# Thirty-two output products of a windowed attention, issued at steps from a table instead of in clusters of four

## The chip, the cores and the metric

The kernel runs on one core of a Trainium2 chip. The metric is the device time of one execution in microseconds (us), the median of several runs. TensorE (PE in the profile; PEld are its weight loads) multiplies, VectorE (DVE), ScalarE (ACT) and GpSimd (POOL) compute elementwise, and SyncE (SP) issues nearly all DMAs. Each engine works through its own queue in the order in which the program gave it the instructions.

## The reference, cut to what matters

Two attentions over 2048 positions, 576 columns and 32 heads of 18, whose outputs stand side by side. A looks at eight positions, two apart; B looks at all. All tensors are float32.

```
def _A_ref(x, wqkv, wo):
    q, k, v = ...                       # x @ wqkv, 32 heads of 18
    idx = pos[:, None] - (arange(8) * 2)[None, :]
    logits = einsum("bhsd,bhswd->bhsw", q, k[idx]) * scale     # masked where idx < 0
    o = einsum("bhsw,bhswd->bhsd", softmax(logits), v[idx])
    return o.reshape(1, 2048, 576) @ wo
def _B_ref(x, wqkv, wo):
    p = softmax(einsum("bhqd,bhkd->bhqk", q, k) * scale)
    return einsum("bhqk,bhkd->bhqd", p, v).reshape(1, 2048, 576) @ wo
return concatenate([a, b], axis=-1)
```

## The kernel before, in words

**Two stages.** In the first, some 415 us, the projections x @ wqkv of both attentions are made. The second is a loop over 512 steps, which this text numbers 0 to 511 as the kernel does. It is B's attention: 8 groups of 4 heads, each with 4 blocks of 512 query positions, make 32 blocks, and a block has 16 steps, one for each tile of 128 keys. So step 16m is the first step of block m.

**One step on each engine.** `score` makes four score matmuls (L229), one for each head, into four PSUM banks that are used in turn (the ring "scores"), and ScalarE takes each through exp into SBUF (L235). Beside three of the four, on the other half of TensorE's rows, runs a matmul of a "maximum" piece (L159), for a later block, into one of three other banks (the ring "else"); VectorE reduces each to its maximum (L166). The order of the pieces alternates: in odd steps they stand beside heads 0, 1 and 2, in even ones beside 0, 1 and 3. When all pieces of a block are done, VectorE makes one more reduction (`least`, L173). Then `weigh` multiplies the exps of the step before with the values and adds them up in the PSUM tile `po` (L701), which holds the sums of a whole block: its first group starts the sum anew, its last one ends it.

**The end of a block.** The sums of the block that ends are complete in step 16m, as `weigh` is one step late. There `finish` has ScalarE copy `po` to SBUF (L710). That copy stands in ScalarE's queue behind the four exps of step 16m and ahead of those of step 16m+1, and the first `weigh` of the next block, in step 16m+1, waits for it. What follows is put on an agenda of later steps: the denominators go out by DMA in step 16m+1 (`den<-o`, L733), VectorE inverts them in step 16m+8 (L734), they go to DRAM (`drec<-den`, L735) and back spread over rows (`rec<-drec`, L736, step 16m+13), and GpSimd multiplies (L737, step 16m+18), rounds and subtracts (L738, L739).

**Attention A beside it.** A is worked through in eight parts of 256 positions (`local(j)`, j from 0 to 7), each of which starts 54 steps after the one before, at step 10 + 54j; times within a part are counted from that step. `arrange` (L822) rearranges q, k and v in DRAM by three large DMAs of many small rows, for j = 4 at the steps 206 to 208. `fetch` (L830) loads them. GpSimd makes the logits in nine turns of a multiplication and an addition (L841, L845) and one last addition (L848). VectorE takes the maximum over the window in three halvings (`am`, L859, due at 31, 32 and 33), GpSimd subtracts it (L865), ScalarE makes the exps (L868, due at 35), VectorE sums them in three halvings (`as`, also L859, due at 36, 37 and 38) and inverts the sums (L875), GpSimd multiplies (`share`, L878, due at 39) and then weighs the values in nine turns (L884 to L887). The result goes to DRAM (`put`) and comes back turned (`get`, L909 and L911, six DMAs into the tiles `at0`, `at1` and `ahl`, of each of which there is one).

**The output products.** For each part, `get(n)` loads one of two tiles of 128 positions, and for each there are two products with `wo`, of 288 columns each: 32 in all. `finished(h)`, when its agenda step p comes, puts the product on the list `inside`, and the scores loop takes it from there in step p + 1, ahead of head 2 or head 3. A product (`sums_of_a`, which calls `beside`) is 27 matmuls in pairs on the two halves of the rows (L1010) with two more maximum pieces in between; it takes one bank of each ring. Then ScalarE copies one of its two sums to the tile `y` (L927) and VectorE adds the other (L928). Six steps after its second product's agenda step, a tile is stored.

Of the kernel before, what the change touches and what calls it, by code (L numbers as in the profile page):

```python
# [43 lines left out]
GAP = 54  # L44

A_FROM = 10


def ap(t, *dims):
# [4 lines left out]
def rows(t, *dims):  # L54

    return bass.AP(tensor=t.tensor, offset=t.offset, ap=[list(d) for d in dims])
# [3 lines left out]
def two_attentions(ctx: ExitStack, tc, xa, wa, woa, xb, wb, wob, out):  # L60
# [53 lines left out]
    def plan(start, pieces):  # L114
        for n, f in pieces:
            agenda[start + n].append(f)
# [222 lines left out]
    with (tc.tile_pool(name="x", bufs=1, side="right") as xp,  # L339
# [104 lines left out]
        if True:  # L444
# [195 lines left out]
            for k in range(2, 14):  # L640
                n = 46 if k == 2 else 36 + 4 * k
# [7 lines left out]
            def leave_a(c, b, n, ps):  # L649
                o = xp.tile([128, 512], F32, name="ohi", bufs=4)  # L650
                nc.scalar.activation(o[:n], ps, AF.Copy)  # L651
                load(da[128 * c : 128 * c + n, HALO + 512 * b : HALO + 512 * b + 512], o[:n])
# [23 lines left out]
            for c, b in order:  # L676
                n = min(128, 3 * D - 128 * c)
                work_list.append(((b % 2, ws[c][0], xas[b][0], slice(0, n), every),
                                  lambda ps, n=n: ps[:n], lambda ps, c=c, b=b, n=n: leave_a(c, b, n, ps)))
# [135 lines left out]
    def local(j):  # L815
# [4 lines left out]
        def arrange(n):  # L820
            wide = (HALO if n else 0) + SUB
            load(rows(dparts[j][n][0, 0], (wide, D), (D * wide, 4), (1, wide)),  # L822
                 rows(da[D * n, HALO + p0 + SUB - wide :], (HALO + S, D), (SUB, 4), (1, wide)))


        def fetch(nm):
            halo = 0 if nm == "q" else HALO
            n = DH * (halo + SUB)
            t = st[nm] = work.tile([128, DH, halo + SUB], F32, name="akv" if halo else "aq", bufs=2 if halo else 1)
            load(ap(t, (1, n)), rows(dparts[j]["qkv".index(nm)][0, 0], (n, 128), (1, n)))  # L830
# [49 lines left out]
        def weighted(c):  # L880
            if c == 0:
                st["o"] = work.tile([128, DH, SUB], F32, name="ao", bufs=1)
            at = wide()
            nc.gpsimd.tensor_mul(at, ap(st["lg"], (0, 2), (SUB, W), (1, SUB)), window(st["v"], c))  # L884
            nc.gpsimd.tensor_add(at[:, :, :4], at[:, :, :4], at[:, :, 4:])  # L885
            nc.gpsimd.tensor_add(at[:, :, :2], at[:, :, :2], at[:, :, 2:4])
            nc.gpsimd.tensor_add(st["o"][:, 2 * c : 2 * c + 2], at[:, :, 0], at[:, :, 1])  # L887
# [10 lines left out]
        def put(i):  # L898
            load(rows(dao[j, i, 0, 0], (DH * SUB, 128), (1, DH * SUB)),
                 ap(st["parts"][i].bitcast(F32), (1, DH * SUB)))  # L900

        def get(n):
            st["x"] = []
            st["n"] = n
            last = work.tile([128, 128], F32R, name="ahl", bufs=1)
            for i in range(2):
                t = work.tile([128, 4, 128], F32R, name=f"at{i}", bufs=1)
                for s in range(2):
                    load(t.bitcast(F32)[:, :, SUB * s : SUB * s + SUB],  # L909
                         dao[j, i, 2 * n + s, :512].rearrange("(c p) n -> p c n", p=128))  # L910
                load(last.bitcast(F32)[64 * i : 64 * i + 64].rearrange("p (s n) -> p s n", s=2),  # L911
                     rows(dao[j, i, 2 * n, 512], (SUB, 64), (D * SUB, 2), (1, SUB)))
                st["x"].append([t[:, c] for c in range(4)])
            st["x"].append(last)

        def finished(h):
            inside.append(lambda: sums_of_a(h))

        def sums_of_a(h):
# [3 lines left out]
            if h == 0:  # L923
# [6 lines left out]
        pieces = [(0, lambda: fetch("q")), (1, lambda: fetch("k")), (28, lambda: fetch("v")), (33, lower),  # L930
                  (35, exponents), (39, share), (60, upper), (61, rest), (64, lambda: put(0)), (66, lambda: put(1))]
# [3 lines left out]
        for c in range(DH // 2):  # L935
            pieces.append((5 + 5 * c // 2, lambda c=c: match(c)))
            pieces.append((39 + 5 * c // 2, lambda c=c: weighted(c)))
        at = A_FROM + GAP * j - 24

        at = max(at, STEPS * (at // STEPS) + 14) - A_FROM - GAP * j  # L940
        for n in range(3):
            pieces.append((at + n if j else n - 7, lambda n=n: arrange(n)))
        for n, (at, ends) in enumerate(((70, (78, 80)), (81, (87, 89)))):
            pieces.append((at, lambda n=n: get(n)))
            for h in range(2):
                pieces.append((ends[h], lambda h=h: finished(h)))
                producing.add(A_FROM + GAP * j + ends[h] + 1)
            pieces.append((ends[1] + 6, lambda n=n: load(out[p0 + 128 * n : p0 + 128 * n + 128, :D], ys["a", j, n])))
# [141 lines left out]
    for j in range(NJ):  # L1090
        plan(A_FROM + GAP * j, local(j))
    for g in range(1, NG):
# [39 lines left out]
    while step < ALL:  # L1132
        n, kt = divmod(step, NT)
# [51 lines left out]
```

## Time and profile before

| what | value |
|---|---|
| time before, median of 3 runs | 1646.38 us (1645.86 to 1647.27) |
| time of the profiled execution | 1646.54 us |
| its span, first to last instruction | 1644.8 us |
| granted TensorE clock | 0.999 |
| busy: PE / DVE / ACT / POOL | 1633.1 / 1397.0 / 1221.9 / 959.2 us |

The time of the profiled execution is 1.74 us more than its span, and 0.16 us more than the median. The busy time of PE is modelled, so that a matmul that waits for a short while is not seen in it: how long a step takes is read better from the starts of successive L701 groups in the timeline, since each step has one. The timeline merges neighbouring instructions of one line; "x8" is one step's group, four matmuls that count twice each. In brackets behind a row stands how long the engine was idle before it, and what ended that.

### The profile page before, as it was taken

To read this page: it belongs to the slowest core of one execution; us is meant where nothing else is said; L and a number is where in the kernel's file an instruction comes from. 1 tells how busy PE (TensorE), PEld (TensorE's weight loads), DVE (VectorE), ACT (ScalarE), POOL (GpSimd) and SP (SyncE) were. 2 spreads that over 40 slices of the span, in tenths; PEclk is the share of its full clock that TensorE was granted. 3 is DMA by queue.
4 is the path that set the end of the run, shared out by engine and by line. 5 is a ranking of instruction groups with operands and counts; after the bars stand their busy time and mean duration, and the time that the engine had idled before them with its cause. 6 is when DMAs were issued, how large, how long until landed. Compare 5 with 4: busy or idle time off the path is not lost.

```text
span 1644.8 us, 33745 instructions
## 1 busy us (share of the span) xinstructions
PE 1633.1 (99%) x12906; PEld 935.0 (57%) x12906; DVE 1397.0 (85%) x2366; ACT 1221.9 (74%) x2419; POOL 959.2 (58%) x792
## 2 busy tenths in 40 slices
PE   9999999999999999999999999999999999999998
PEld 7999879998433444444344344344344344445676
DVE  5199989999899989889889899889899989888533
ACT  6314432111899998998998998998998998998554
POOL 2306642210195995994994994994995996940000
PEclk9999999999999999999999999999999999999999
DMA  8837955522515347157139325716526132033201
GB/s 252 238 113 204 257 165 140 134 87 90 95 48 100 98 120 135 54 139 143 53 93 161 82 77 130 147 65 122 134 79 117 65 107 78 21 114 123 101 37 59
DMA packets 188353, 188.22 MB, mean 114 GB/s; under 512 B 118384, under 2 KB 132208, under 8 KB 186464
## 3 DMA queue, kind: packets, MB, share of 16 engines
q1 hardware_dynamic: 183328, 174.53, 40.9%
q0 software_dynamic: 4032, 10.63, 3.0%
q8 instruction: 101, 1.65, 0.4%
q10 hardware_dynamic: 832, 0.92, 0.2%
q14 instruction: 60, 0.49, 0.1%
HBM read 113.16 MB, written 88.12 MB: 122 GB/s over the span
## 4 chain that ended last, share of the span: by engine, by line
PE 96%; DMA 2%; DVE 1%; ACT 0%; POOL 0%; issue 0%; SPq 0%; ACTq 0%; POOLq 0%; DVEq 0%
PE po L701 30%; PE bank L229 25%; PE bank L322 16%; PE bank L159 13%; PE bank L1010 7%; PE bank L259 5%; DMA den<-o 1%; DVE mx L166 1%; DMA dqk<-ohi 0%; POOL xlo L370 0%; DMA first<-xb 0%; DVE am L859 0%; SPq L363 0%; DMA out<-y 0%; PE bank L985 0%
## 5 line engine op out<-in xcount | busy, mean ns | idle before, releaser
L166 DVE TENSOR_REDUCE mx<-bank 128x1 f32<-128x512 f32 x2048 | 1288.1, 683 | 144.6 <-PE bank L159 115.8
L235 ACT ACTIVATE e<-bank 128x512 f32<-128x512 f32 x2048 | 1060.2, 613 | 94.3 <-PE bank L229 51.0
L159 PE MATMUL bank<-ks,qs 54*128 54x512 f32 x2048 | 752.7, 423 | 2.1 <-DVE mx L166 2.0
L229 PEld LDWEIGHTS bank<-qs,ks 56*128 56x128 f32 x2048 | 331.1, 186 | 454.1 <-ACT e L235 423.6
L229 PE MATMUL bank<-qs,ks 56*128 56x512 f32 x2048 | 582.0, 425 | 0.0
L701 PE MATMUL po<-e,v 128*19 128x512 f32 x4096 | 538.1, 599 | 0.0
L159 PEld LDWEIGHTS bank<-ks,qs 54*128 54x128 f32 x2048 | 340.8, 185 | 15.6 <-DVE mx L166 7.6
L841 POOL TENSOR_TENSOR pr<-aq,akv 128x1024 f32<-128x1024 f32 x72 | 158.4, 2201 | 28.1 <-DMA akv<-dpart 25.6
L701 PEld LDWEIGHTS po<-e,v 128*19 128x19 f32 x4096 | 70.6, 97 | 182.1 <-issue 171.4
L884 POOL TENSOR_TENSOR pr<-lg,akv 128x1024 f32<-128x1024 f32 x72 | 158.1, 2196 | 0.6
L845 POOL TENSOR_TENSOR pr<-pr 128x1024 f32<-128x1024 f32 x64 | 152.5, 2382 | 5.0
L651 ACT ACTIVATE ohi<-bank 128x512 f32<-128x512 f32 (+1 forms) x56 | 30.5, 595 | 148.3 <-issue 116.9
L322 PE MATMUL bank<-xlo,ahi 64*128 64x512 f32 (+1 forms) x448 | 117.9, 389 | 1.4 <-POOL xlo L370 1.4
L322 PE MATMUL bank<-xhi,alo 64*128 64x512 f32 (+1 forms) x448 | 116.1, 388 | 0.0
L322 PE MATMUL bank<-xhi,ahi 64*128 64x512 f32 (+1 forms) x448 | 113.7, 388 | 1.1 <-ACT ohi L651 1.1
L885 POOL TENSOR_TENSOR pr<-pr 128x512 f32<-128x512 f32 x72 | 92.3, 1282 | 5.6
L370 POOL TENSOR_TENSOR alo<-raw,ahi 128x512 fp32r<-128x512 f32 (+1 forms) x14 | 17.6, 1254 | 121.1 <-ACT ahi L369 86.7
L463 POOL TENSOR_TENSOR olo<-olo,ohi 128x512 fp32r<-128x512 f32 x36 | 46.1, 1294 | 63.8 <-ACT ohi L462 58.4
L737 POOL TENSOR_TENSOR o<-o,rec 128x512 f32<-128x512 f32 x29 | 37.2, 1284 | 64.3 <-DMA rec<-drec 35.4
L322 PEld LDWEIGHTS bank<-xlo,ahi 64*128 64x128 f32 (+1 forms) x448 | 67.2, 182 | 7.6 <-POOL xlo L370 2.5
L322 PEld LDWEIGHTS bank<-xhi,alo 64*128 64x128 f32 (+1 forms) x448 | 65.8, 182 | 5.3
L322 PEld LDWEIGHTS bank<-xhi,ahi 64*128 64x128 f32 (+1 forms) x448 | 63.8, 181 | 7.2 <-ACT ohi L651 1.5
(197 smaller groups left out, 1790.5 us busy)
## 6 DMA issues: line engine op xcount, KB each, us to landing
do<-n SPq DMA_DIRECT2D x28, 512.0 KB
da<-ohi SPq DMA_DIRECT2D x52, 256.0 KB
dpart<-da SPq DMA_DIRECT2D x16, 702.0 KB
akv<-dpart SPq DMA_DIRECT2D x16, 702.0 KB
out<-y SPq DMA_DIRECT2D x32, 288.0 KB
qs<-dqk SPq DMA_DIRECT2D x30, 288.0 KB
ks<-dqk SPq DMA_DIRECT2D x30, 288.0 KB
at<-dao SPq DMA_DIRECT2D x64, 128.0 KB
```

The costliest lines, as they stand in the source:

```text
L159: nc.tensor.matmul(ps, qs[at, b, p, 128 * t : 128 * t + 128], ks[at, p, 512 * k : 512 * k + 512], start=True, stop=True)
L166: nc.vector.tensor_reduce(mx[:, r, p, t, k : k + 1], ps, axis=AX.X, op=ALU.max)
L229: nc.tensor.matmul(ps, ks[at, p, 128 * kt : 128 * kt + 128], qs[at, b, p], start=True, stop=True)
L235: nc.scalar.activation(e, ps, AF.Exp, scale=SCALE)
L259: nc.tensor.matmul(ps, a, b, start=c == i == 0, stop=c == 4 and i == 1)
L322: nc.tensor.matmul(ps, a, b, start=start, stop=stop)
L701: nc.tensor.matmul(po[32 * i : 32 * i + 19], vs[g][:, kt, 19 * i : 19 * i + 19], es[i], start=kt == 0, stop=kt == NT - 1)
L841: nc.gpsimd.tensor_mul(pr, ap(st["q"][:, 2 * c], (SUB, 2), (0, W), (1, SUB)), window(st["k"], c))
L845: nc.gpsimd.tensor_add(st["pr"], st["pr"], pr)
L884: nc.gpsimd.tensor_mul(at, ap(st["lg"], (0, 2), (SUB, W), (1, SUB)), window(st["v"], c))
L885: nc.gpsimd.tensor_add(at[:, :, :4], at[:, :, :4], at[:, :, 4:])
L1010: nc.tensor.matmul(ps, a, b, start=start, stop=stop)
```

## The change

The four products of a part stood at fixed places, 78, 80, 87 and 89 steps after the part's start, with the loads at 70 and 81. Now their agenda steps are in a table, counted over the whole loop, one row for each part. Of its 32 entries 24 are a multiple of 16, so that these products run in step 16m+1: for m = 6 to 28 and m = 30. The load for a tile's products is due eight steps ahead of the first of them, or one step after the second product of the tile before, whichever is later. The steps that count as having two more maximum pieces (`producing`) and the store follow the table.

```
+MADE = ((88, 96, 112, 128), (144, 160, 176, 192), (201, 208, 224, 240), (250, 256, 272, 288),
+        (304, 320, 336, 352), (361, 368, 384, 400), (412, 416, 432, 448), (466, 468, 475, 480))
...
-        for n, (at, ends) in enumerate(((70, (78, 80)), (81, (87, 89)))):
-            pieces.append((at, lambda n=n: get(n)))
+        made = [p - A_FROM - GAP * j for p in MADE[j]]
+        for n, ends in enumerate((made[:2], made[2:])):
+            pieces.append((max(ends[0] - 8, made[1] + 1 if n else 0), lambda n=n: get(n)))
             for h in range(2):
                 pieces.append((ends[h], lambda h=h: finished(h)))
                 producing.add(A_FROM + GAP * j + ends[h] + 1)
```

Before, the products ran in the steps 89, 91, 98, 100 and then 54 steps later each time, up to 467, 469, 476 and 478. No instruction is added or removed: each engine's queue holds the same instructions in another order, and from step 489 on the order is as before.

## The prediction
> **What bounds the kernel now.** First the page: engines, and the chain of work that ended last.
>
> ```profile
> PE 1633.1 (99%) x12906; PEld 935.0 (57%) x12906; DVE 1397.0 (85%) x2366; ACT 1221.9 (74%) x2419; POOL 959.2 (58%) x792
> ...
> PE 96%; DMA 2%; DVE 1%; ACT 0%; POOL 0%; issue 0%; SPq 0%; ACTq 0%; POOLq 0%; DVEq 0%
> ```
>
> TensorE is the path almost throughout. As no matmul is added or removed, only time in which TensorE waits can come or go. Its busy time hides short waits, so I read the timeline of PE and took the distance between the starts of successive L701 groups as the length of a step. Around the end of block 7 (steps 112 to 114) it says:
>
> ```profile
> 667.39 1.05 PE L701 MATMUL po<-e,v 128*19 128x512 f32 x8
> 669.51 1.05 PE L701 MATMUL po<-e,v 128*19 128x512 f32 x8
> 671.81 1.05 PE L701 MATMUL po<-e,v 128*19 128x512 f32 x8
> ...
> 668.73 0.63 ACT L710 ACTIVATE o<-po 128x512 f32<-128x512 f32 x1
> 669.21 7.31 ACT L235 ACTIVATE e<-bank 128x512 f32<-128x512 f32 x14
> ```
>
> A plain step is 2.12 us; the one from 669.51 to 671.81, step 114 = 16·7 + 2, is 2.30. The second view, ScalarE over the same time, says why: the copy starts at 668.73 and the next exp at 669.21, so a queued activation takes 0.48 us of ScalarE. Four make 1.92, 0.2 less than a step. The copy puts ScalarE 0.48 late, one step gives back 0.2, and in the next TensorE waits for score banks. The first such step is 18 and the last 482:
>
> ```profile
> 456.42 1.05 PE L701 MATMUL po<-e,v 128*19 128x512 f32 x8
> 458.69 1.05 PE L701 MATMUL po<-e,v 128*19 128x512 f32 x8
> ...
> 1518.09 1.05 PE L701 MATMUL po<-e,v 128*19 128x512 f32 x8
> 1520.37 1.05 PE L701 MATMUL po<-e,v 128*19 128x512 f32 x8
> ```
>
> They are 2.27 and 2.28 long. Of the ends m = 1 to 30, 26 show it; 146, 210, 306 and 370 don't, as a product stood in step 16m or 16m + 1.
>
> **The copies.** Step 305 = 16·19 + 1 already has a product where the table puts 24:
>
> ```profile
> 1106.35 1.05 PE L701 MATMUL po<-e,v 128*19 128x512 f32 x8
> 1110.59 1.05 PE L701 MATMUL po<-e,v 128*19 128x512 f32 x8
> 1112.70 1.05 PE L701 MATMUL po<-e,v 128*19 128x512 f32 x8
> ...
> 1110.17 0.41 ACT L927 ACTIVATE y<-bank 128x288 f32<-128x288 f32 x1 [0.90 <-PE bank L1010]
> ```
>
> It takes 4.24 us and the step after it 2.11, a plain one. A product so adds 2.12 to its step, and ScalarE, with the copy behind it, still has 0.90 us idle ahead of the product's own copy. So there the copy of the sums is free. Six ends stay uncovered (m = 1 to 5 and 29): 20 stalls of 0.17 go, **−3.4 us**.
>
> On this size the Trainium skill speaks otherwise: its page "ScalarE: Activation LUTs" ("What ACT_TABLE_LOAD costs") gives an activation 186 ns and 0.833 ns an element, with 93 ns of overlap between neighbours, an estimate of 0.52 us for 512 elements. By that figure ScalarE would have 0.04 us to spare in a step, a copy would cost TensorE nearly all its time, and 20 would bring over 9 us, with a sum below of some −11 instead of −4.65; the spacing of 0.48 and the step of 2.30 decide against it.
>
> **GpSimd's lead.** Moving products changes how long other work has between two steps. For part 1, two products (steps 89, 91) stood between `share` of part 0 and `am` of part 1; now one.
>
> ```profile
> 625.97 1.28 POOL L848 TENSOR_TENSOR lg<-pr 128x512 f32<-128x512 f32 x1
> 632.72 1.29 POOL L865 TENSOR_TENSOR lg<-lg,am 128x512 f32<-128x512 f32 x1 [5.46 <-DVE am L859]
> ...
> 628.14 0.42 DVE L859 TENSOR_TENSOR am<-lg 128x256 f32<-128x256 f32 x1
> ...
> 526.80:627.20 100.40, 96.66 (x70) 1.00 0.39 101
> ```
>
> GpSimd works without a break from 526.8 to the end of the logits at 627.25 (in the last row, busy time by stretches: 96.66 of 100.4 with 70 instructions; the rest is small change between them), so that this end stays. VectorE reaches `am` at 628.14 now, and by one product's 2.12 earlier after: 626.02. It waits 1.2 us; behind `am` stand the reductions that free banks for the maximum pieces, so TensorE stops for most of it. I take **+1.15** (0.8 to 1.4). For the later parts three or four products lie in that stretch instead of two, so the lead grows.
>
> **The `as` step.** The first `as` halving comes in an odd step, where the third piece is early and VectorE has least to spare. Before, from part 1 on a product ran just ahead of it.
>
> ```profile
> 518.35 1.05 PE L701 MATMUL po<-e,v 128*19 128x512 f32 x8
> 520.63 1.05 PE L701 MATMUL po<-e,v 128*19 128x512 f32 x8
> ...
> 519.59 0.42 DVE L859 TENSOR_TENSOR as<-lg 128x256 f32<-128x256 f32 x1
> ...
> 641.82 1.05 PE L701 MATMUL po<-e,v 128*19 128x512 f32 x8
> 643.95 1.05 PE L701 MATMUL po<-e,v 128*19 128x512 f32 x8
> ```
>
> Part 0, without a product, pays 2.28 − 2.12 = 0.16; part 1, with it, nothing (2.13). After, all parts but 3 (product in 209) lose that cover: 6 × 0.16 = **+1.0** (0 to 1.0).
>
> **The long stall at step 218.** The largest wait of the loop is one DMA:
>
> ```profile
> 864.78 0.92 SPq L909 DMA_DIRECT2D at<-dao  x2
> ...
> 867.69 2.68 SPq L911 DMA_DIRECT2D ahl<-dao  x1
> ...
> 872.18 0.35 SPq L735 DMA_DIRECT2D drec<-den  x1
> ...
> 882.95 0.58 SPq L736 DMA_DIRECT2D rec<-drec  x1
> 883.59 12.82 SPq L822 DMA_DIRECT2D dpart<-da  x3
> 896.50 5.74 SPq L733 DMA_DIRECT2D den<-o  x1
> ...
> 909.99 0.25 DVE L734 RECIPROCAL den<-den 128x16 f32<-128x16 f32 x1 [2.44 <-DMA den<-o]
> ...
> 908.35 1.05 PE L701 MATMUL po<-e,v 128*19 128x512 f32 x8
> 912.46 1.30 PE L701 MATMUL po<-e,v 128*19 128x512 f32 x8
> 915.70 1.45 PE L701 MATMUL po<-e,v 128*19 128x512 f32 x8
> ```
>
> SP is blocked for 12.82 us by `arrange` of part 4, `den` of step 209 is issued behind it and lands at 909.99, VectorE stands, and TensorE loses 4.11 − 2.11 = 2.0 and 3.24 − 2.11 = 1.1, and 0.4 in the step after: 3.5. `arrange` itself waits for nothing that is computed; it starts late because `rec` stands ahead of it, which waits for `drec`, which SP reached only after the second load of part 2 (864.78 to 870.37). That load waited for the product in step 199. In the new table it is due at 216, after all this. SP then comes to `drec` when the inverse is made, some 3 us earlier against the steps, and its landing, with one load less ahead of it (128 × 576 values of 4 bytes, twice), comes earlier too. Against that, part 2's first load moves from 188 to 193, the very step of a product that it must wait for, and what SP has behind it is late. From both: the stall ends between nothing and its whole; I take **−2.2** (−3.5 to 0).
>
> **VectorE against GpSimd.** An `am` of 256 columns takes 0.42 (row at 628.14), but:
>
> ```profile
> 1002.30 1.37 DVE L859 TENSOR_TENSOR am<-lg 128x256 f32<-128x256 f32 x1
> ...
> 1002.11 1.28 POOL L737 TENSOR_TENSOR o<-o,rec 128x512 f32<-128x512 f32 x1 [5.35 <-DMA rec<-drec]
> ...
> 1003.34 1.05 PE L701 MATMUL po<-e,v 128*19 128x512 f32 x8
> 1006.19 1.05 PE L701 MATMUL po<-e,v 128*19 128x512 f32 x8
> ...
> 1376.77 1.06 PE L701 MATMUL po<-e,v 128*19 128x512 f32 x8
> 1382.04 1.05 PE L701 MATMUL po<-e,v 128*19 128x512 f32 x8
> ```
>
> It ends when GpSimd's multiplication does, and the step after it, 259 (1003.34 to 1006.19), is 2.85, 0.73 over. Step 422 (1376.77 to 1382.04), a product step with two late `am` halvings ahead of it, is 5.27 instead of 4.24: 1.03. In the first case the multiplication waited for `rec`, which SP issued behind a load whose product stood in step 253; that load is now due at 264, `rec` comes earlier, and the multiplication is over by then. In part 7 GpSimd is further ahead. I take two thirds of 1.76, **−1.2** (−1.8 to +1, as other meetings can form).
>
> **The sum.** −3.4 + 1.15 + 1.0 − 2.2 − 1.2 = −4.65. From the profiled 1646.54 that is 1641.9; this execution is 0.16 above the median, so I predict **1641.7**. The moved loads themselves I cost at nothing: seven of eight second loads are due eight steps (17 us) before their product, where 81 to 87 left six; if that cover were short, TensorE would wait for the landing.
>
> **Rivals.** A measurement of this kernel tells about 0.2% (3.3 us) from no change: below 1643.1 is faster, above 1649.7 slower.
>
> *The side effects eat it.* The copies go, but `den` stays as late and the meetings of VectorE and GpSimd only change place: −3.4 + 1.15 + 1.0 = −1.25, **1645.1**. For it: without the two uncertain gains the sum stays under the bound. Against it: the load that blocked SP is gone from that place. Chance 0.19.
>
> *The product doesn't cover the copy*, so the change doesn't do what it says: the product's own copy to `y` also runs on ScalarE in that step. Then the 3.4 stays: −4.65 + 3.4 = −1.25, **1645.1** too. Step 305 speaks against it. Chance 0.03.
>
> *SP late from step 193: slower.* The load due in 193 waits for that step's product, about 3 us, then issues for 5.6 (864.78 to 870.37), then come nine small DMAs at 0.35 or more (as `drec`), then `den` of block 12: some 12 us after the step's start. If the queue is then as full as at 896.50, where landing took 13.5 us from the issue, `den` lands at 25.5, and the inverse is wanted at 4.24 + 7 × 2.12 + 0.25 = 19.3. That is 6 us, and the stall at 218 stays: −1.25 + 6 = +4.75, **1651.1**. From 4.6 us late on it is past the bound. Against it: in the same queue, some steps later, such a load went out whole in 5.6 us and `drec` followed 1.8 us behind its end, so a queue as full as at 896.50 is not to be expected. Chance 0.10.
>
> **How the numbers follow.** My forecast has 0.68. The best of every term gives −3.4 + 0.8 + 0 − 3.5 − 1.8 = −7.9: low end 1638.5. The worst of the uncertain ones (1.4, 1.0, 0, +1) gives 0.0; the two rivals without change of sign lie at 1645.1, and 1646.0 takes them in and leaves out what is left of the upper side, with the third, some 0.15. Faster 0.68, within the bound 0.19 + 0.03 = 0.22, slower 0.10.
>
> **What would show it.** In the profile after: steps 16m + 2 for m = 6 to 28 and 30 at 2.11 and 16m + 1 at 4.23; a VectorE `am` of part 1 that starts where L848 ends, with some 1 us lost in steps 96 and 97; `den` of step 209 issued earlier against the steps; 0.16 at the first `as` of parts 1, 2, 4 to 7. Wrong would be: 2.28 still in those steps, or a long inverse (L734) wait anywhere, step 200 first.

## The result: 0.2% slower, and where it went

| kernel | time, median us | ratio to the kernel before, 95% interval |
|---|---|---|
| before | 1647.10 (14 runs) | |
| changed | 1651.01 (14 runs) | 1.0020 (1.0012 to 1.0029) |

The forecast was 1641.7, and 1638.5 to 1646.0: the change went the other way. The profiled execution of the changed kernel took 1651.53 us, its span is 1649.8 (1644.8 before).

I read its profile as the one before, by the starts of successive groups of the values' matmul (now L704; lines behind the table stand three or four further down). First the end of block 7, which the prediction showed with 2.30 us in step 114. The four rows are the steps 111 to 114, with a product in 113:

```profile
664.78 1.05 PE L704 MATMUL po<-e,v 128*19 128x512 f32 x8
666.89 1.05 PE L704 MATMUL po<-e,v 128*19 128x512 f32 x8
671.13 1.05 PE L704 MATMUL po<-e,v 128*19 128x512 f32 x8
673.23 1.05 PE L704 MATMUL po<-e,v 128*19 128x512 f32 x8
```

The product step takes 4.24 and the step after it 2.10: the copy costs nothing. So it is at all 24 ends that the table covers; the stall is left at 18, 34, 66, 82 and 466 (at 50 another wait took its place in step 49). The gain that the change was argued from is there in full.

Now the place of the longest stall, step 218, in the timeline of TensorE, then VectorE, then SP:

```profile
906.34 1.05 PE L704 MATMUL po<-e,v 128*19 128x512 f32 x8
916.25 1.91 PE L704 MATMUL po<-e,v 128*19 128x512 f32 x8
920.10 1.24 PE L704 MATMUL po<-e,v 128*19 128x512 f32 x8
922.39 1.05 PE L704 MATMUL po<-e,v 128*19 128x512 f32 x8
...
867.42 0.24 DVE L737 RECIPROCAL den<-den 128x16 f32<-128x16 f32 x1
...
913.23 0.25 DVE L737 RECIPROCAL den<-den 128x16 f32<-128x16 f32 x1 [7.66 <-DMA den<-o]
...
850.86 0.93 SPq L912 DMA_DIRECT2D at<-dao  x2
...
865.26 0.43 SPq L952 DMA_DIRECT2D out<-y  x1
...
872.62 0.35 SPq L738 DMA_DIRECT2D drec<-den  x1
...
887.79 0.57 SPq L739 DMA_DIRECT2D rec<-drec  x1
888.41 10.25 SPq L825 DMA_DIRECT2D dpart<-da  x3
898.76 7.56 SPq L736 DMA_DIRECT2D den<-o  x1
```

From 906.34 to 916.25 are 9.91 us, then 3.85 and 2.29: 9.7 us over three plain steps of 2.12, where the kernel before lost 3.5. VectorE waited 7.66 instead of 2.44 for `den` (the inverse at 867.42, of the block before, waited for nothing). TensorE lost more than VectorE waited, and the busy times by stretches say why; behind the length of the stretch the columns are PE, PEld, DVE, ACT and POOL, then TensorE's granted clock, the DMA engines' share and GB/s:

```profile
907.50:910.00 2.50, 0.32 (x1) 0.00 (x1) 0.00 (x0) 0.92 (x2) 2.34 (x3) 1.00 1.01 88
910.00:913.00 3.00, 0.00 (x0) 0.00 (x0) 0.00 (x0) 0.00 (x0) 2.84 (x4) 0.55 0.20 21
913.00:916.00 3.00, 1.92 (x6) 1.32 (x6) 2.77 (x6) 0.66 (x2) 2.84 (x4) 0.50 0.31 101
916.00:919.00 3.00, 3.00 (x13) 0.97 (x14) 1.09 (x3) 1.09 (x3) 2.92 (x2) 0.50 0.81 183
919.00:922.00 3.00, 3.00 (x19) 1.15 (x18) 2.00 (x4) 2.18 (x5) 2.84 (x4) 0.74 0.81 235
```

TensorE stood from about 908, its clock fell to half, and stayed there until about 920, six us after work came back. A group that takes 1.05 us elsewhere takes 1.91 at 916.25. The Trainium skill has this rule on its page "TensorE: Matmul & The Clock Gate" ("What's actually happening"): after an idle window of some 3.4 us the array gets half its clock, and only a busy window gives it back. The trace agrees on the half, 0.50, and on a return only after some six us of work. It doesn't show the idle window of 3.4 us: TensorE's last matmul ended at 907.82, and a mean of 0.55 over 910 to 913 puts the fall at some 910.3, 2.5 us later. The kernel before had the half clock too, shorter:

```profile
913.00:916.00 3.00, 3.00 (x19) 1.31 (x15) 2.21 (x5) 1.76 (x5) 2.84 (x4) 0.52 0.93 312
```

By steps 2 to 486 of the two profiled executions, over plain steps of 2.115 us and product steps of 4.23 and 4.21 (these are sums over the rows of L701 and L704):

| where | before | after | difference |
|---|---|---|---|
| ends of blocks that the table covers (20 stalls) | 3.4 | 0 | −3.4 |
| steps 212, 213, 259, 373, 422 | 3.0 | 0 | −3.0 |
| steps 218 to 220 | 3.5 | 9.7 | +6.2 |
| step 97 | 0 | 1.3 | +1.3 |
| steps 104 to 106 | 0.2 | 0.9 | +0.7 |
| first `as`, steps 101, 155, 263, 317, 425 | 0 | 0.9 | +0.9 |
| all others | 3.3 | 3.8 | +0.5 |
| sum | 13.4 | 16.6 | +3.2 |

The spans differ by 5.0. Some 1.6 of that came before the loop's second step, where the two kernels have the same instructions in the same order. Over the ten profiles of this study, all with that same first stage, step 2 begins between 422.7 and 426.7: that part is scatter of the single execution, and it isn't the change. The last 0.2 are the product steps themselves: before, about half of the 32 took 4.21 instead of 4.23, after it three.

Two more rows of the forecast's list. Part 1's `am` waits for the logits, 1.36 us, and the product step 97 (628.49 to 634.06) is 5.57 long:

```profile
628.49 1.05 PE L704 MATMUL po<-e,v 128*19 128x512 f32 x8
634.06 1.05 PE L704 MATMUL po<-e,v 128*19 128x512 f32 x8
...
629.05 0.43 DVE L862 TENSOR_TENSOR am<-lg 128x256 f32<-128x256 f32 x1 [1.36 <-POOL lg L851]
```

And a second `den`, of block 6, is late where the forecast named none; it was issued behind part 2's `arrange`:

```profile
651.17 1.05 PE L704 MATMUL po<-e,v 128*19 128x512 f32 x8
654.20 1.05 PE L704 MATMUL po<-e,v 128*19 128x512 f32 x8
...
651.73 0.25 DVE L737 RECIPROCAL den<-den 128x16 f32<-128x16 f32 x1 [1.08 <-DMA den<-o]
```

### The profile page after: what moved, and what is told of

It reads as the page before. It is cut to its first block, busy times and chain, and to the rows that moved or that the text cites. A ratio compares the mean times of both kernels' runs of the same rounds, so it can differ in the third digit from the quotient of the medians.

```text
span 1649.8 us, 33746 instructions
## 1 busy us (share of the span) xinstructions
PE 1632.9 (99%) x12906; PEld 951.6 (58%) x12906; DVE 1392.9 (84%) x2366; ACT 1224.0 (74%) x2419; POOL 960.1 (58%) x792
## 4 chain that ended last, share of the span: by engine, by line
PE 90%; POOL 6%; DMA 1%; DVE 1%; issue 1%; ACT 0%; SPq 0%; POOLq 0%; ACTq 0%; DVEq 0%
PE po L704 27%; PE bank L232 22%; PE bank L325 16%; PE bank L162 13%; PE bank L1014 7%; PE bank L262 5%; POOL pr L844 1%; POOL pr L887 1%; POOL pr L848 1%; DMA den<-o 1%; DVE mx L169 1%; POOL pr L888 1%; POOL pr L889 0%; DMA dqk<-ohi 0%; PE bank L478 0%
## 5 line engine op out<-in xcount | busy, mean ns | idle before, releaser
L232 PE MATMUL bank<-qs,ks 56*128 56x512 f32 x2048 | 573.0, 426 | 0.0
L704 PE MATMUL po<-e,v 128*19 128x512 f32 x4096 | 538.4, 600 | 0.0
L162 PEld LDWEIGHTS bank<-ks,qs 54*128 54x128 f32 x2048 | 341.3, 185 | 18.0 <-DVE mx L169 11.4
L704 PEld LDWEIGHTS po<-e,v 128*19 128x19 f32 x4096 | 70.6, 97 | 185.7 <-issue 182.9
L325 PE MATMUL bank<-xlo,ahi 64*128 64x512 f32 (+1 forms) x448 | 111.2, 390 | 0.2 <-POOL xlo L373 0.2
L325 PEld LDWEIGHTS bank<-xlo,ahi 64*128 64x128 f32 (+1 forms) x448 | 62.5, 183 | 3.2 <-POOL xlo L373 1.0
```

The source lines that it names most:

```text
L162: nc.tensor.matmul(ps, qs[at, b, p, 128 * t : 128 * t + 128], ks[at, p, 512 * k : 512 * k + 512], start=True, stop=True)
L232: nc.tensor.matmul(ps, ks[at, p, 128 * kt : 128 * kt + 128], qs[at, b, p], start=True, stop=True)
L325: nc.tensor.matmul(ps, a, b, start=start, stop=stop)
L704: nc.tensor.matmul(po[32 * i : 32 * i + 19], vs[g][:, kt, 19 * i : 19 * i + 19], es[i], start=kt == 0, stop=kt == NT - 1)
```

## The experiments

Two theories stood against each other. **Queue**: the change gains by the products' places and loses it all, and more, at `den` of step 209, which SP issues late because part 2's first load now waits in its queue for a product of its own step. **Spread**: products that stand alone cost more than products in clusters, and the stall at 218 is one of the forms this takes.

The ratios below are to runs of the kernel before that were made beside each run: their median is 1648.64 us (20 runs) for the first four kernels, which ran on one chip, and 1647.47 (23 runs) for the other four, on another.

**Part 4's `arrange` moved away from `den`, in both kernels.** In each, one line:

```
-        at = max(at, STEPS * (at // STEPS) + 14) - A_FROM - GAP * j
+        at = (180 if j == 4 else max(at, STEPS * (at // STEPS) + 14)) - A_FROM - GAP * j
```

In the changed kernel:

> The changed kernel with one more edit: the three DMAs of arrange for part 4 are due at steps 180 to 182 instead of 206 to 208, so that the denominators of step 209 are not issued behind them. Theory (queue): the whole loss of the change is the wait of VectorE for these denominators in step 218, 9.7 us of TensorE in the changed kernel (8.65 and 1.06 over a plain step) against 3.5 before. Then steps 218 and 219 are plain, TensorE's clock stays at 1.0 around them, and the time is 1651.0 - 9.7 = 1641.3 (1640 to 1643), 0.35% under the kernel before. Rival (moved, not removed): the DMA work is the same and another den, rec or load is late instead; the time stays at 1647 to 1651. Rival (spread): the products cost more where they stand now than in clusters, beside the stall; then 1644 or more.

Measured: 1640.54 us, 0.9956 of the kernel before (0.9941 to 0.9971). The steps 218 and 219 in its timeline are plain, and the clock is whole:

```profile
904.62 1.05 PE L704 MATMUL po<-e,v 128*19 128x512 f32 x8
906.73 1.05 PE L704 MATMUL po<-e,v 128*19 128x512 f32 x8
908.85 1.05 PE L704 MATMUL po<-e,v 128*19 128x512 f32 x8
...
910.00:915.00 5.00, 5.00 (x37) 2.25 (x37) 4.31 (x8) 4.85 (x10) 4.76 (x5) 1.00 0.03 12
```

In the kernel before:

> The kernel before with the same edit alone: arrange of part 4 at 180 to 182. Theory (queue): steps 218 and 219 lose their 3.5 us, 1647.1 - 3.5 = 1643.6 (1642.5 to 1645). The difference to the changed kernel with this edit is then what the change does beside that one stall: by the steps of its trace -3.4 (copies), +1.3 (step 97), +0.7 (step 106 against 104 and 105), +0.9 (as), -2.8 (steps 212, 259, 373, 422), about -3. Rival (moved): no change of time.

Measured: 1643.92 us, 0.9969 (0.9959 to 0.9980). With that one stall out of both, the changed kernel is 3.4 us below the kernel before, on the same chip and about as its steps add up (8.1 over plain, against 11.9). The intervals of the two ratios overlap, so the size of this gain rests on the steps as well as on the medians. With that, the change's other effects are a gain, and the stall at 218 turns it. The rival "moved, not removed" falls for the changed kernel, in whose trace no other step took the stall over. In the kernel before the time falls too, but its trace has a wait that wasn't there: VectorE waits 1.61 us for a later `den`, and step 282 loses 1.2. As the profiled execution was the slowest of the nine (1646.78), it stays open whether this wait belongs to the edit.

**The product ahead of part 2's first load.** One entry of the table:

```
-        (144, 160, 176, 192)
+        (144, 160, 176, 184)
```

> The changed kernel with one table entry changed, 192 to 184: the first load of part 2 stays due at 193, but the product that it must wait for is then eight steps back. Theory (wait): SP stands at that load until the product of step 193 has run (850.86, 2.7 us into it), and what follows, eight small DMAs, den and five qs loads, is late; without it drec lands earlier, arrange of part 4 starts by some 5 us earlier against the steps, and steps 218 and 219 lose 3.5 us or less instead of 9.7; 1651.0 - 6.2 + 0.2 (one copy uncovered) = 1645 (1641 to 1646). Rival (order): it is the place of the load ahead of the qs loads, not the wait, that counts: the stall stays at 7 to 10 us, 1649 to 1652.

Measured: 1641.65 us, 0.9958 (0.9943 to 0.9974). The load is still due at 193, but SP reaches it early and nothing holds it there. Its rows, and the chain behind it up to `den`, with VectorE's inverse and the step 218:

```profile
836.84 0.35 SPq L952 DMA_DIRECT2D out<-y  x1
837.63 0.98 SPq L912 DMA_DIRECT2D at<-dao  x2
...
869.44 0.35 SPq L738 DMA_DIRECT2D drec<-den  x1
...
880.80 0.57 SPq L739 DMA_DIRECT2D rec<-drec  x1
881.42 12.09 SPq L825 DMA_DIRECT2D dpart<-da  x3
893.61 7.05 SPq L736 DMA_DIRECT2D den<-o  x1
...
907.24 0.25 DVE L737 RECIPROCAL den<-den 128x16 f32<-128x16 f32 x1
...
908.09 1.05 PE L704 MATMUL po<-e,v 128*19 128x512 f32 x8
910.21 1.05 PE L704 MATMUL po<-e,v 128*19 128x512 f32 x8
```

The load goes out at 837.63 instead of 850.86. Then `drec` is issued right behind its inverse and `rec` follows 11.4 us later, instead of 15.2, `arrange` starts at 881.42 instead of 888.41 (8.7 us earlier, counted from each trace's step 200), and the inverse waits for nothing; TensorE has no stall there at all (908.09 to 910.21). That is better than I had expected, which was up to the old 3.5 and 1645 us. The product's place, through the wait, is the cause, and not the load's place among the other loads: all loads stay where they were due. One thing else moves with the product, the store of its tile (`out<-y`, 288 KB): in the changed kernel it goes out at 865.26, ahead of `drec`, and here at 836.84, ahead of the load. How much of the shorter way from `drec` to `rec` is due to the store, this run doesn't tell.

**The same spread beside no copy.** With `arrange` of part 4 at 180, so that the queue's stall is out of the way:

```
+MADE = ((88, 92, 108, 124), (140, 156, 172, 188), (201, 204, 220, 236), (250, 252, 268, 284),
+        (300, 316, 332, 348), (361, 364, 380, 396), (410, 412, 428, 444), (466, 468, 475, 476))
```

> The changed kernel with arrange of part 4 at 180 to 182, and with the products that the table puts at multiples of 16 moved four steps ahead (two of them by other small numbers, so that no step has two): as widely spread, but none beside a copy of the sums. Theory (cover): all ends of blocks m = 1 to 30 show the 0.17 again, 24 more than in the run with the table, +4.1; step 97 is free, as two products lie ahead of am of part 1 again, -1.2: 2.9 us over that run (1.5 to 4). Rival (spread): the gain of steps 16m + 2 comes from having no clusters, and the time is that of the run with the table or less.

Measured: 1647.5 us, 0.9990 (0.9980 to 1.0001), 7.0 over the run with the table. Its trace shows the 24 stalls of some 0.17, here step 114 again (671.49 to 673.78: 2.29):

```profile
671.49 1.05 PE L704 MATMUL po<-e,v 128*19 128x512 f32 x8
673.78 1.06 PE L704 MATMUL po<-e,v 128*19 128x512 f32 x8
...
753.77 1.50 DVE L862 TENSOR_TENSOR am<-lg 128x256 f32<-128x256 f32 x1
...
753.70 1.29 POOL L742 TENSOR_TENSOR n<-o,n 128x512 fp32r<-128x512 f32 x1
```

So the cover is what gains, and not the spread. The sign is as expected, the size is over it, by two things that the expectation lacked: steps 106 and 107 lose 3.7 (0.9 and 0.0 in the changed kernel), behind a wait of VectorE of 2.35 us for `den`, and in step 151 an `am` of 1.50 us, beside a subtraction of GpSimd (753.70), costs 1.0. The steps add up to 5.9 over the run with the table, and its first stage was 0.8 later in the profile.

**Step 97 and step 106.** Three runs on the changed kernel with `arrange` of part 4 at 180: part 0's second product back ahead of `am`, part 2's `arrange` earlier, and both.

```
-MADE = ((88, 96, 112, 128), ...
+MADE = ((88, 90, 112, 128), ...
```

> The changed kernel with arrange of part 4 at 180 to 182, and the second product of part 0 back from 96 to 90 (its step 97 to 91). Theory (GpSimd's lead): the 1.3 us lost in step 97 come from am of part 1, which comes a product earlier than GpSimd's logits; with the product ahead of am again they go, and the copy of block 6 costs its 0.17 in step 98. But the denominators of that block land at their own time, not at a step's, so the wait in step 106 (1.03 us in the run with the table) grows by what was saved, to some 2.1: the time stays at 1640.5 (1640 to 1641.5). Rival (steps apart): 106 stays at 1.0, and the time is 1639.4.

Measured: 1642.45 us, 0.9968 (0.9954 to 0.9982), a little over the range expected. In its timeline `am` no longer waits, and `den` does, for longer:

```profile
628.83 0.41 DVE L862 TENSOR_TENSOR am<-lg 128x256 f32<-128x256 f32 x1
...
651.06 0.25 DVE L737 RECIPROCAL den<-den 128x16 f32<-128x16 f32 x1 [2.47 <-DMA den<-o]
...
649.13 1.05 PE L704 MATMUL po<-e,v 128*19 128x512 f32 x8
653.52 1.91 PE L704 MATMUL po<-e,v 128*19 128x512 f32 x8
657.18 1.05 PE L704 MATMUL po<-e,v 128*19 128x512 f32 x8
...
650.00:655.00 5.00, 3.71 (x19) 1.12 (x15) 3.87 (x8) 2.85 (x6) 4.76 (x5) 0.85 0.69 186
655.00:660.00 5.00, 5.00 (x34) 2.10 (x30) 3.16 (x6) 3.37 (x7) 4.68 (x7) 0.81 0.16 53
```

Step 97's 1.3 is gone. VectorE's wait for `den` is 2.47 instead of 1.23 in the run with the table: what was saved ahead of a fixed landing is waited out behind it, as expected. TensorE however loses 3.8 there, not 2.1, because the longer stop let the clock fall (0.85 and 0.81 over five us each), and the run is slower by steps (9.3 us over plain, against 8.1).

```
-        at = (180 if j == 4 else max(at, STEPS * (at // STEPS) + 14)) - A_FROM - GAP * j
+        at = ({2: 84, 4: 180}[j] if j in (2, 4) else max(at, STEPS * (at // STEPS) + 14)) - A_FROM - GAP * j
```

> The changed kernel with arrange of part 4 at 180 to 182 and that of part 2 at 84 to 86 instead of 94 to 96. Theory (queue): the wait in step 106 is the denominators of step 97 behind these three DMAs, as in step 218; it goes (-1.0), step 97 keeps its 1.3, and the time is 1639.5 (1638.5 to 1640.5). Rival (moved): the loads around step 89 come late instead, and step 89 or 97 is over a us longer than now; no gain or a loss.

Measured: 1640.5 us, 0.9959 (0.9946 to 0.9973). In the trace step 106 is plain, 97 keeps its 1.2, and no other step grew by more than 0.2: the steps add up to 5.8 instead of 8.1, of which 1.0 is step 106 and 0.6 step 49, which differs by as much between traces of kernels that are alike up to there. The median shows no gain on the run with one `arrange` moved (the ratios are 0.9959 and 0.9956, on two chips), and its interval of 2 us either way can't tell one of this size.

Both edits together:

> Both edits: arrange of parts 2 and 4 at 84 and 180, and the second product of part 0 in step 91. Theory: 97 and 106 both lose their waits, +0.17 for one copy: 1640.5 - 1.3 - 1.0 + 0.2 = 1638.4 (1637.5 to 1640), 0.6% under the kernel before, and no step from 50 to 480 is more than 0.4 over a plain one. Rival (moved): some other late load takes their place, 1640 or more.

Measured: 1638.26 us, 0.9942 (0.9923 to 0.9962), the lowest median of all. Neither step 97 nor 106 is over a plain step; 98 has its copy's 0.18, and the largest excess from step 50 to 480 is 0.34 (step 421).

**VectorE against GpSimd.** The kernel before, with one load and its two products moved:

```
-        for n, (at, ends) in enumerate(((70, (78, 80)), (81, (87, 89)))):
+        for n, (at, ends) in enumerate(((70, (78, 80)), (84, (91, 93)) if j == 3 else (81, (87, 89)))):
```

> The kernel before, with the second load of part 3 due at 256 instead of 253 and its two products at 263 and 265 instead of 259 and 261. Theory (SP's order): step 259 loses 0.74 us because rec of step 253 stands behind that load, which waits for the product of step 253; GpSimd's multiplication then runs beside am. With the load behind rec the multiplication starts where the logits end, the first am of part 4 takes 0.42 instead of 1.37, and step 259 is plain. Rival (chance meeting): am still takes over 1 us.

Measured in a single run: 1643.85 us. In its trace the multiplication starts where the logits end, and `am` takes 0.42:

```profile
995.58 1.29 POOL L848 TENSOR_TENSOR lg<-pr 128x512 f32<-128x512 f32 x1
996.82 1.29 POOL L737 TENSOR_TENSOR o<-o,rec 128x512 f32<-128x512 f32 x1
...
1000.27 0.42 DVE L859 TENSOR_TENSOR am<-lg 128x256 f32<-128x256 f32 x1
```

Step 259 is plain, so in this one trace the meeting went with the order in SP's queue. The same trace also shows what I can't explain by this edit: step 218, which comes before it, lost 1.3 us instead of 3.5, and 212 nothing. VectorE waited 1.76 us for `den` instead of 2.44, and TensorE's clock stayed whole (the columns as above):

```profile
909.42 0.25 DVE L734 RECIPROCAL den<-den 128x16 f32<-128x16 f32 x1 [1.76 <-DMA den<-o]
...
913.00:916.00 3.00, 3.00 (x22) 1.42 (x22) 2.52 (x5) 2.53 (x5) 2.84 (x4) 1.00 0.92 324
```

A wait shorter by 0.7 us, in another execution of instructions that are the same up to there, so became 2.2 us in the steps.

## Why the prediction was wrong, point by point

**The copies: right.** −3.4 expected and measured, at the steps named, and the run beside no copy brings the stalls back.

**GpSimd's lead: right.** +1.15 expected in steps 96 and 97, 1.3 measured in 97; with the product back ahead of `am` it is gone.

**The `as` step: right.** 0.16 at six steps expected, 0.18 or 0.19 at five of them; the sixth, 371, is plain.

**VectorE against GpSimd: the mechanism was right, the size too small.** −1.2 expected, two thirds of what the steps 259 and 422 lost; both went whole, −1.8, and with them 212, 213 and 373, −1.2, which the prediction didn't name. In the profile before, a halving on VectorE is long in each of them beside an instruction of GpSimd, as here in step 212:

```profile
894.08 1.01 DVE L859 TENSOR_TENSOR as<-as 128x64 f32<-128x64 f32 x1
...
893.72 1.29 POOL L737 TENSOR_TENSOR o<-o,rec 128x512 f32<-128x512 f32 x1 [7.29 <-DMA rec<-drec]
```

In the changed kernel no halving in those steps is over 0.5 us. The run with part 3's load moved shows the reason for step 259; for the others it is argued from the same order and wasn't tried one by one. Step 212 was plain in that run too, ahead of its edit, so that meeting comes and goes between executions.

**The long stall at step 218: this step failed.** The prediction has there "SP then comes to `drec` when the inverse is made, some 3 us earlier against the steps, and its landing, with one load less ahead of it [...], comes earlier too", and −2.2. Measured: +6.2. It saw that part 2's first load moves to the very step of a product that it must wait for, and weighed this as less than the second load's going. But behind the first load stood eight small DMAs, `den`, and five large loads of q, which before had gone out by then, and the store of the tile of step 193's product (at 865.26; before, that tile was stored at 774.22). They came late together. SP came to `drec` 5.0 us after the inverse was made (867.66 to 872.62; 3.2 before), which is 1.7 later against the start of step 200, and `drec` had them ahead of it: `rec` could follow 15.2 us after it (872.62 to 887.79), against 10.8 before. Together that is 6.1 us, by which `arrange` starts later against the steps; that the loads and the store are what held `drec` is argued from the order of issue. From there the chain is that of the prediction: `rec`, `arrange`, `den`, the inverse. The table entry 184 takes the wait away and with it the whole stall: there SP comes to `drec` when the inverse is made, 3.2 us earlier against the steps than before, as the prediction had it. What it had wrong is the price of the first load's wait.

**The third rival had the mechanism and the sign** ("SP late from step 193"), but looked for its price at `den` of block 12, which VectorE took without a wait, and left the stall at 218 as it was. Its point of decision was sought at the first `den` behind the load; the one that counted stood 16 steps later, behind `arrange`. That its 1651.1 lies so near the measured 1651.01 is luck.

**A term that was missing: the clock.** The prediction priced a wait at its length or less (the 1.2 us of `am`, the 6 us of the third rival). Over the traces here, waits of VectorE ahead of this inverse from 1.02 to 1.76 us (five of them) cost TensorE 0.9 to 1.3, with the clock whole; waits of 2.35, 2.44 and 2.47 cost 3.5 to 3.8, and one of 7.66 cost 9.7, and behind these four the clock was at half for three us or more. The 3.5 of the kernel before, read off the steps, were put down to the wait alone and had this in them.

**The second `den`, step 106: missing.** The prediction spoke of `arrange` only at part 4. Part 2's stands at 94 to 96, ahead of `den` of step 97, and two product steps that lay between `den` and its inverse had moved away: +0.7. With that `arrange` moved ahead, step 106 is plain.

## What to carry to other kernels

A moved instruction that loads into a tile still in use is a wait put into its queue, and everything behind it in that queue moves too; so follow the queue until the next thing that has a due time, not only to the next one. Where two waits stand in line for the same late landing, taking the first away is no gain until the second is gone. A stop of TensorE can cost more than its length: behind waits of VectorE of 2.35 us and more the clock here was at half for three us or more, behind those of up to 1.76 us it was not.

## What the runs showed of the hardware that was not expected

The first stage, the same in all kernels, ended between 422.7 and 426.7 us in ten profiles. That scatter is as large as the effect of the change; the sum over steps, taken within one trace, told effects of 1 us that the medians couldn't.

In the kernel before, the clock fell to 0.52 (913 to 916) after a stretch in which TensorE stood idle for only 1.0 us at once and was busy for 2.2 of the three us from 910 to 913. The Trainium skill's page "TensorE: Matmul & The Clock Gate" ("What's actually happening") speaks of an idle window of 3.4 us; here less than that sufficed.
